# Backward attention: dO times O summed to one column a head group, added to dP group by group on VectorE

## The chip, the cores and the metric

The kernel runs on one core of a Trainium2 chip. The metric is the device time of one execution in microseconds; the time before is the median of three runs. A core has five engines that run side by side, each with its own queue of instructions in a fixed order: TensorE (in the profile PE for its matmuls and PEld for its weight loads), VectorE (DVE), ScalarE (ACT), GpSimd (POOL) and SyncE (SP, which here only issues DMAs). An instruction that needs another engine's result waits for a semaphore, and everything behind it in its engine's queue waits with it. Matmuls write into PSUM, from which VectorE or ScalarE must copy the result out (an evacuation) before the buffer can be used again.

## What is computed

A transformer block, forward and backward in one launch: a LayerNorm with a modulation from a condition vector, an attention with 32 heads over 64 segments of 32 rows with 8 memory rows carried from segment to segment, and a gated feed-forward network. The outputs are the block's output and eleven gradients. The part that matters is the attention of one segment, and its gradient:

```python
q = jnp.einsum('btd,dhe->bhte', h, Wq)
k = jnp.einsum('btd,dhe->bhte', h, Wk)
v = jnp.einsum('btd,dhe->bhte', h, Wv)
scores = jnp.einsum('bhqe,bhke->bhqk', q, k) * scale
scores = jnp.where(mask[None, None], scores, -1000000000.0)
p = _softmax(scores, axis=-1)
o = jnp.einsum('bhqk,bhke->bhqe', p, v)
o = jnp.einsum('bhte,hed->btd', o, Wo)
mem = o[:, :M, :].copy()
...
_out, _vjp = jax.vjp(_f, A_x, A_mem0, A_Wq, A_Wk, A_Wv, A_Wo, B_w_gate, B_w_up, B_w_down, c, w_mod)
_grads = _vjp(grad_out)
```

Going backward, with dO the gradient of a head's output and P its softmax, the gradient of the values is dV = P^T dO. With dP = dO V^T, the gradient of the scores is dS = scale * P * (dP - D), where D is one number for each query row, the sum of dO times O over the row. Then dQ = dS K and dK = dS^T Q. The gradient of the memory rows goes to the segment before, so the 64 segments run one after the other, from the last to the first.

## The kernel before

The kernel runs in stages; the change lies in the one of the backward attention, `phase4`. Its loop takes the 64 segments in turn. The 32 heads are packed three to a group of 120 columns (3 heads of 40 rows), which gives 11 groups, and the groups are worked on in three parts, `pi` = 0, 1, 2, of 4, 4 and 3 groups. A part of 4 groups of 128 columns in float32 is one PSUM bank.

What one segment does, in the order of the code:

- The incoming gradient `dyT` is multiplied with Wo (`col_pass`, L255) and turned (`turn`, L1480) to give dO for each head, `dOT`. `prod` (L1578) multiplies `dOT` into the stored O on VectorE, in place.
- `grad_mm("dVT", ...)` gives the products of dV^T, gv0, gv1 and gv2, one a part; `dp` (L1593) gives dO V^T into `dp_ps`; `dost(2)` transposes the last groups of `dOT`.
- `ds` (L1601) subtracts D: it multiplies the product dO times O by a matrix of minus ones (`negones`), 120 columns wide, into the same PSUM buffer as `dp`, so that each of the 120 columns has D taken off. One instruction of VectorE for each part (L1603) multiplies this by the scale and by P and writes `dS`.
- The head products `dht(dVT, WvT, ...)` (L215) add dV^T times Wv into `dh_ps`. They use the array in strips of 32 columns, four heads side by side. Then follow gv2 and gr0, gr1, gr2, the products of the dV rows, which `rv_out` copies out of PSUM: part 0 and 2 on ScalarE, part 1 on VectorE.
- `dstt(0)` to `dstt(2)` transpose `dS` on TensorE (L1526); part 1 is evacuated by VectorE, 0 and 2 by ScalarE, into `dST`.
- Three products of dK^T (`gks`), evacuated by VectorE into `dKT`, and three of dQ^T, evacuated by ScalarE into `dQT`. Then the head products with Wk (`dht(dKT, WkT, pi)`), the rest of those with Wv, and those with Wq (L223).
- The sums are folded (`fold_split`, `split_pair`, `fold_sum`), which gives the memory gradient that the next segment starts from.

Every fourth segment also evacuates a product of the rows outside the memory into `RBd` on VectorE, ahead of its `ds`, and does a second small transpose in the middle.

Two things set the order of the work. At the end of the loop `self.pin(i0)` ties the instructions of each engine to the order in which the code issues them, so nothing overtakes. And most PSUM tiles of the loop come from one pool, `psp`, with six buffers under one tag; which buffer a tile gets, and so whose evacuation its first matmul has to wait for, is decided by the framework when the program is built. `ps_f32` and `ps_b16` take from it. The pool `psb` holds the long sums `dh_ps` apart from these.

Of the kernel before, what the change touches and what calls it, by code (L numbers as in the profile page):

```python
# [8 lines left out]
F32 = mybir.dt.float32  # L9
AF = mybir.ActivationFunctionType  # L10
ALU = mybir.AluOpType
# [29 lines left out]
class K:  # L41
# [1356 lines left out]
    def phase4(self):  # L1398
        nc, tc, cfg, io = self.nc, self.tc, self.cfg, self.io
        D, DC, H, E, L, M, T, G, NS = cfg.D, cfg.DC, cfg.H, cfg.E, cfg.L, cfg.M, cfg.T, cfg.G, cfg.NS  # L1400
        GW = 128
# [4 lines left out]
        with self.p4_ctx as ctx:  # L1406
            WqT, WkT, WvT, WoT, negones = self.WqT, self.WkT, self.WvT, self.WoT, self.negones
# [4 lines left out]
            sb2 = ctx.enter_context(tc.tile_pool(name="p4s2", bufs=2, reuse_waits="tile"))  # L1412
# [3 lines left out]
            PG = 4  # L1416
            PW = PG * GW

            def ps_f32(name):
                return psp.tile([128, PG, GW], F32, name=name, tag="p")  # L1420
# [23 lines left out]
            def part3(t, pi):  # L1444
                return t[:, pi * PW:min((pi + 1) * PW, G * GW)].rearrange("p (g x) -> p g x", x=GW)
# [75 lines left out]
            def transposes_part(src, pi, w=GW, m=128):  # L1521
                ps = ps_b16("tps")
                n = min(PG, G - pi * PG)
                for j in range(n):
                    g = pi * PG + j
                    nc.tensor.transpose(ps[:, j, 0:m], src[0:m, g * w:g * w + GW], self.ident[0:m, 0:m])  # L1526
                return ps[:, 0:n, 0:m]
# [32 lines left out]
            for s in reversed(range(NS)):  # L1560
# [11 lines left out]
                VT, OT, Pst, Kst, Qst = ld["VT"], ld["OT"], ld["Pst"], Kst_t, Qst_t  # L1572
                dS, dST, dOst = dSs[0], dSTs[0], dOst_t
                dVT, dKT, dQT = dXTs["dVT"][0], dXTs["dKT"][0], dXTs["dQT"][0]
# [13 lines left out]
                def dp(pi):  # L1588
                    ps = dps[pi] = ps_f32("dp_ps")
                    n = min(PG, G - pi * PG)  # L1590
                    for j in range(n):
                        g = pi * PG + j
                        nc.tensor.matmul(ps[:, j, 0:120], lhsT=dOT[:, g * 120:g * 120 + GW], rhs=VT[:, g * GW:g * GW + 120],  # L1593
                                         start=(j == 0), stop=False, skip_group_check=True)

                def ds(pi):
                    ps = dps[pi]
                    n = min(PG, G - pi * PG)
                    for j in range(n):
                        g = pi * PG + j  # L1600
                        nc.tensor.matmul(ps[:, j, 0:120], lhsT=OT[:, g * GW:(g + 1) * GW], rhs=negones[:, 0:120],  # L1601
                                         start=False, stop=True, skip_group_check=True)
                    nc.vector.scalar_tensor_tensor(out=part3(dS, pi)[:, :, 0:120], in0=ps[:, 0:n, 0:120],  # L1603
                                                   scalar=cfg.scale, in1=part3(Pst, pi)[:, :, 0:120],
                                                   op0=ALU.mult, op1=ALU.mult)

                def grad_part(nm, lh, rh, xt, pi, eng):
                    grad_out(nm, xt, pi, eng, grad_mm(nm, lh, rh, pi))

                def grad_mm(nm, lh, rh, pi):  # L1610
                    ps = ps_f32("g_ps")
                    n = min(PG, G - pi * PG)
                    for j in range(n):
                        g = pi * PG + j
                        w = GW if nm == "dV" else 120
                        nc.tensor.matmul(ps[:, j, 0:w], lhsT=lh[:, g * GW:(g + 1) * GW], rhs=rh[:, g * GW:g * GW + w],  # L1616
                                         start=True, stop=True)
                    return ps

                def grad_out(nm, xt, pi, eng, ps):  # L1620
                    self.evac(eng, part3(xt, pi)[:, :, 0:120], ps[:, 0:min(PG, G - pi * PG), 0:120])
                    if pi == NP - 1 and nm != "dVT":
                        rows = rxp.tile([128, G, 128], BF16, name="rows_x")
                        nc.sync.dma_start(rows[:], xt[:, :], transpose=True)
                        dram = {"dKT": self.DKR, "dQT": self.DQR}[nm][s]
                        row_stores.append(lambda: nc.gpsimd.dma_start(dram, rows[:]))
# [3 lines left out]
                def rv_out(pi, eng, ps):  # L1630
                    n = min(PG, G - pi * PG)
                    self.evac(eng, rv_rows[:, pi * PG:pi * PG + n, :], ps[:, 0:n, :])

                def dstt(pi):
                    ps = transposes_part(dS, pi, m=120)
                    self.evac("dve" if pi == 1 else "act", part3(dST, pi)[:, :, 0:120], ps)
# [32 lines left out]
                gv0 = grad_mm("dVT", dOst, Pst, 0)  # L1669
                prod(0)  # L1670
                dp(0)
                prod(1)
                dp(1)
                prod(2)
                dp(2)
                gv1 = grad_mm("dVT", dOst, Pst, 1)
                grad_out("dVT", dVT, 0, "act", gv0)
                if b_done:
                    b_done()
                dost(2)  # L1680
                grad_out("dVT", dVT, 1, "act", gv1)
                ds(0)
                ds(1)
                ds(2)
                self.pop_later()
                dht(dVT, WvT, 0)
# [3 lines left out]
                gr1 = grad_mm("dV", Pst, dOst, 1)  # L1690
# [11 lines left out]
                    dO_tails(s - 1)  # L1702
                grad_out("dVT", dVT, 2, "act", gv2)
                rv_out(0, "act", gr0)
                rv_out(1, "dve", gr1)
                dstt(0)
                rv_out(2, "act", gr2)
                row_stores.append(lambda s=s, rows=rv_rows: nc.gpsimd.dma_start(self.DVR[s], rows[:]))
                dstt(1)
                dstt(2)  # L1710
                gks = [grad_mm("dKT", Qst, dS, pi) for pi in range(NP)]
                load_rows(Qst_t, self.QST, s - 1)
# [22 lines left out]
                g = s // 4  # L1735
# [428 lines left out]
```

## Time and profile before

| | us |
|---|---|
| median of 3 runs (3080.75 to 3086.59) | 3083.49 |
| the profiled execution's own time | 3080.64 |
| its span, first to last instruction | 3078.9 |
| mean granted TensorE clock over the span | 0.991 |
| backward attention loop, first to last row of L1601 | 1539.2 to 2493.1 |
| VectorE's dS (L1603), 192 instructions, busy | 111.4 |
| VectorE's wait ahead of L1603 | 19.2 |
| matmuls of L1601, 704 instructions, each | 0.216 |

The lines of the profile are read like this. A group of instructions has its line in the code, engine, operation, what it writes and reads (`out<-in`), partitions by elements and type, how often, then the busy time in us, the mean length of one in ns, and the idle time of the engine just before them with what ended it. A line of the timeline has start and length in us, and several like instructions in a row are merged into one with their count. Line 63 and line 61 are those of the helper `evac`, so evacuations are told apart by their tiles. Matmuls overlap: each takes 0.216 us from start to end, but the next starts long before that.

### The profile page before, as it was taken

What the parts mean: (1) busy time and instruction counts of PE and PEld (TensorE: products, weight loads), DVE (VectorE), ACT (ScalarE), POOL (GpSimd) and SP (SyncE); (2) the same over time, 40 slices, a digit from 0 to 9 for tenths busy, and PEclk for the clock granted to TensorE, in tenths of its full rate; (3) what the DMA queues carried; (4) which work ended last, traced back from release to release, by engine and by line L of the source; (5) the groups of instructions that cost most, each with busy time, mean ns of one, the idle gap of its engine ahead of it and who ended that gap; (6) DMA issues with size and microseconds to landing.
All of it is one profiled execution on the core that took longest, in us unless ns stands there. A gap on an engine that the chain in (4) does not pass through costs nothing.

```text
span 3078.9 us, 106050 instructions
## 1 busy us (share of the span) xinstructions
PE 2985.9 (97%) x43769; PEld 1821.5 (59%) x43845; DVE 1613.0 (52%) x3799; ACT 1254.4 (41%) x3056; POOL 1386.1 (45%) x2960
## 2 busy tenths in 40 slices
PE   6999999999999799989899999999999999999999
PEld 3666666666665444445577777777777754445455
DVE  4556656665655788742255555555555632322221
ACT  2555555555555433322155555555555520111011
POOL 3666767667766222211244444444444422333322
PEclk8999999999999899999999999999999999999999
DMA  8888788788778799997599999999999998666574
GB/s 300 217 215 204 204 209 217 203 214 212 206 202 255 199 229 231 225 282 254 176 232 246 244 247 246 245 248 244 248 243 245 253 278 278 201 194 221 188 236 149
DMA packets 845992, 703.54 MB, mean 229 GB/s; under 512 B 544354, under 2 KB 717954, under 8 KB 845124
## 3 DMA queue, kind: packets, MB, share of 16 engines
q1 hardware_dynamic: 714196, 486.69, 62.7%
q0 software_dynamic: 60656, 148.64, 15.1%
q10 hardware_dynamic: 70656, 61.41, 6.4%
q8 instruction: 345, 5.65, 0.8%
q14 instruction: 139, 1.14, 0.1%
HBM read 294.93 MB, written 276.35 MB: 186 GB/s over the span
## 4 chain that ended last, share of the span: by engine, by line
PE 45%; issue 3%; POOL 1%; DMA 1%; DVE 0%; ACT 0%; SPq 0%; POOLq 0%
PE gps L1954 9%; PE dh_ps L215 8%; PE g_ps L1616 6%; PE pass_ps L255 5%; PE gps5o L1968 5%; PE dhq_ps L223 4%; PE dh_tps L215 3%; PE dp_ps L1593 2%; PE tps L1526 2%; PE dp_ps L1601 1%; PE turn_ps L1480 1%; PE dh_ft L323 1%; POOL out_dram L1958 1%; DMA dhb<-DHA 0%; PE turn_ps L264 0%
## 5 line engine op out<-in xcount | busy, mean ns | idle before, releaser
L1954 PE MATMUL gps<-rows,hrows 128*128 128x512 bf16 (+2 forms) x2124 | 415.6, 355 | 1.9
L1954 PEld LDWEIGHTS <-hrows 128*128 128x128 bf16 x2160 | 211.3, 98 | 204.5
L255 PEld LDWEIGHTS <-hT 128*32 128x32 bf16 x6144 | 158.3, 97 | 168.5 <-DMA Wq<-in_A_Wq_dram 5.5
L1660 POOL COPY dOst<-RAd 96x512 bf16<-96x512 bf16 x128 | 75.5, 613 | 311.4 <-DVE RAd L63 311.2
L63 DVE CAST ot<-gps 128x512 bf16<-128x512 f32 (+3 forms) x76 | 48.1, 633 | 286.9 <-PE gps L1954 188.4
L1958 POOL DMA_DIRECT2D out_dram<-ot x108 | 81.5, 755 | 255.9 <-DVE ot L63 137.2
L61 ACT ACTIVATE ot<-gps 128x512 bf16<-128x512 f32 (+3 forms) x75 | 41.3, 551 | 352.3 <-PE gps L1954 230.7
L909 POOL TENSOR_TENSOR Pst<-Pst,rden 120x1408 bf16<-120x1408 bf16 x63 | 159.7, 2536 | 47.7 <-issue 21.4
L61 ACT ACTIVATE dVT<-g_ps 128x480 bf16<-128x480 f32 (+1 forms) x192 | 104.7, 545 | 95.5 <-PE g_ps L1616 95.1
L63 DVE CAST RA0v<-pass_ps 128x512 bf16<-128x512 f32 x128 | 88.5, 692 | 91.2 <-PE pass_ps L255 85.3
L255 PE MATMUL pass_ps<-Wv,hT 128*32 128x512 bf16 x2048 | 134.2, 382 | 0.0
L215 PE MATMUL dh_ps<-WvT,dVT 128*32 128x512 bf16 x2048 | 133.4, 380 | 0.3 <-DVE RBd L63 0.2
L255 PE MATMUL pass_ps<-Wq,hT 128*32 128x512 bf16 x2048 | 123.3, 383 | 5.3 <-DMA Wq<-in_A_Wq_dram 5.3
L1968 PE MATMUL gps5o<-WoT,rows 128*128 128x512 bf16 x580 | 127.7, 379 | 0.6
L223 PE MATMUL at_ps<-Wo,OT 128*32 128x256 bf16 x4096 | 124.6, 274 | 3.0 <-DMA Wo<-in_A_Wo_dram 3.0
L255 PE MATMUL pass_ps<-Wk,hT 128*32 128x512 bf16 x2048 | 121.6, 379 | 2.2 <-ACT hT L899 1.1
L255 PE MATMUL pass_ps<-WoT,dyT 128*32 128x256 bf16 (+1 forms) x3072 | 122.4, 308 | 0.9 <-ACT dyT L1734 0.9
L223 PE MATMUL dhq_ps<-WqT,dQT 128*32 128x256 bf16 x4096 | 122.9, 273 | 0.0
L215 PE MATMUL dh_ps<-WkT,dKT 128*32 128x512 bf16 x2048 | 122.3, 380 | 0.0
L223 PEld LDWEIGHTS <-dQT 128*32 128x32 bf16 x4096 | 109.6, 97 | 15.9
L1603 DVE SCALAR_TENSOR_TENSOR dS<-dp_ps,Pst_l 128x480 bf16<-128x480 f32 (+1 forms) x192 | 106.1, 608 | 19.2 <-PE dp_ps L1601 19.2
L223 PEld LDWEIGHTS <-OT 128*32 128x32 bf16 x4096 | 103.8, 97 | 18.6 <-issue 6.5
(421 smaller groups left out, 7034.9 us busy)
## 6 DMA issues: line engine op xcount, KB each, us to landing
OSR<-Ost SPq DMA_DIRECT2D x64, 352.0 KB
OT<-OT SPq DMA_DIRECT2D x64, 352.0 KB
VT<-VTr SPq DMA_DIRECT2D x64, 352.0 KB
PS<-Pst SPq DMA_DIRECT2D x64, 352.0 KB
OT_l<-OT SPq DMA_DIRECT2D x64, 352.0 KB
Pst_l<-PS SPq DMA_DIRECT2D x64, 352.0 KB
VT_l<-VT SPq DMA_DIRECT2D x64, 352.0 KB
DVR<-rows_x POOLq DMA_DIRECT2D x64, 352.0 KB, 6.2
```

The lines of the kernel that those rows point to most:

```text
L61: return nc.scalar.activation(out, in_, AF.Copy)
L63: return nc.vector.tensor_copy(out, in_)
L215: self.nc.tensor.matmul(ps[32 * j:32 * j + 32, :], lhsT=lhsT, rhs=w, start=(n < 4), stop=(n >= total - 4), tile_position=(0, 32 * j))
L223: nc.tensor.matmul(ps[32 * j:32 * j + 32, :], lhsT=x[k], rhs=w[k][:, 256 * d:256 * d + 256], start=(n == 0), stop=(n == total - 1), tile_p ...
L255: self.nc.tensor.matmul(ps[32 * j:32 * j + 32, :], lhsT=lhs(c), rhs=rhs, start=(c == 0), stop=(c == DC - 1), tile_position=(0, 32 * j))
L909: nc.gpsimd.tensor_tensor(Pst[0:120, :, :], Pst[0:120, :, :], rden[:, :].unsqueeze(2).to_broadcast([120, G, 128]), op=ALU.mult)
L1603: nc.vector.scalar_tensor_tensor(out=part3(dS, pi)[:, :, 0:120], in0=ps[:, 0:n, 0:120], scalar=cfg.scale, in1=part3(Pst, pi)[:, :, 0:120], ...
L1616: nc.tensor.matmul(ps[:, j, 0:w], lhsT=lh[:, g * GW:(g + 1) * GW], rhs=rh[:, g * GW:g * GW + w], start=True, stop=True)
L1660: nc.gpsimd.tensor_copy(dOst[0:96, 512 * hf:512 * hf + 512], RAd[0:96, 512 * hf:512 * hf + 512])
L1954: nc.tensor.matmul(ps[:, 0:ng * E], lhsT=hrows[:, tp_, c * 128:(c + 1) * 128], rhs=rows[:, tp_, 0:ng * E], start=(tp_ == 0), stop=(tp_ == ...
L1958: nc.gpsimd.dma_start(outw[c * 128:(c + 1) * 128, h0:h0 + 3 * (ng - 1) + 1:3, :], ot[:, 0:ng * E].rearrange("p (h e) -> p h e", e=E))
L1968: nc.tensor.matmul(pss[gg][:], lhsT=src[0][:, src[1], gg * E:(gg + 1) * E], rhs=dyrows[:, tp_, :], start=(tp_ == order[0]), stop=(tp_ == o ...
```

## The change

`dp` closes its sums. `ds` multiplies by one column of minus ones in place of 120 and puts the result, minus D, into column 120 of each group's part of the same PSUM buffer, which `dp` leaves free. VectorE copies these columns of a part (4, 4 and 3) into a small tile `negD`, and then does one instruction for each of the 11 groups: it adds the group's column of `negD` to dP and multiplies by P. The scale is no longer in `dS`; `grad_out` puts it in as it evacuates dK^T (VectorE) and dQ^T (ScalarE), while dV^T is copied as before. `rv_out(1, "dve", gr1)`, the copy of the second part of the dV rows, is issued after `dstt(1)` in place of before `dstt(0)`.

```diff
                         nc.tensor.matmul(ps[:, j, 0:120], lhsT=dOT[:, g * 120:g * 120 + GW], rhs=VT[:, g * GW:g * GW + 120],
-                                         start=(j == 0), stop=False, skip_group_check=True)
+                                         start=(j == 0), stop=True, skip_group_check=True)
 
                 def ds(pi):
                     ps = dps[pi]
                     n = min(PG, G - pi * PG)
                     for j in range(n):
                         g = pi * PG + j
-                        nc.tensor.matmul(ps[:, j, 0:120], lhsT=OT[:, g * GW:(g + 1) * GW], rhs=negones[:, 0:120],
+                        nc.tensor.matmul(ps[:, j, 120:121], lhsT=OT[:, g * GW:(g + 1) * GW], rhs=negones[:, 0:1],
                                          start=False, stop=True, skip_group_check=True)
-                    nc.vector.scalar_tensor_tensor(out=part3(dS, pi)[:, :, 0:120], in0=ps[:, 0:n, 0:120],
-                                                   scalar=cfg.scale, in1=part3(Pst, pi)[:, :, 0:120],
-                                                   op0=ALU.mult, op1=ALU.mult)
+                    nd = sb2.tile([128, PG], F32, name="negD", bufs=3)
+                    nc.vector.tensor_copy(nd[:, 0:n], ps[:, 0:n, 120])
+                    for j in range(n):
+                        g = pi * PG + j
+                        nc.vector.scalar_tensor_tensor(out=dS[:, g * GW:g * GW + 120], in0=ps[:, j, 0:120],
+                                                       scalar=nd[:, j:j + 1], in1=Pst[:, g * GW:g * GW + 120],
+                                                       op0=ALU.add, op1=ALU.mult)
...
                 def grad_out(nm, xt, pi, eng, ps):
-                    self.evac(eng, part3(xt, pi)[:, :, 0:120], ps[:, 0:min(PG, G - pi * PG), 0:120])
+                    to, src = part3(xt, pi)[:, :, 0:120], ps[:, 0:min(PG, G - pi * PG), 0:120]
+                    if nm == "dVT":
+                        self.evac(eng, to, src)
+                    elif eng == "act":
+                        nc.scalar.activation(to, src, AF.Copy, scale=cfg.scale)
+                    else:
+                        nc.vector.tensor_scalar_mul(to, src, cfg.scale)
...
                 rv_out(0, "act", gr0)
-                rv_out(1, "dve", gr1)
                 dstt(0)
                 rv_out(2, "act", gr2)
                 row_stores.append(lambda s=s, rows=rv_rows: nc.gpsimd.dma_start(self.DVR[s], rows[:]))
                 dstt(1)
+                rv_out(1, "dve", gr1)
                 dstt(2)
```

## The prediction

> **What bounds the kernel now.** I read the page's first part, then the stage of the backward attention loop (1537 to 2495 us) as a table of stretches, then one segment in order of time, engine by engine.
>
> ```profile
> PE 2985.9 (97%) x43769; PEld 1821.5 (59%) x43845; DVE 1613.0 (52%) x3799; ACT 1254.4 (41%) x3056; POOL 1386.1 (45%) x2960
> 1540.00:2490.00 950.00, 946.60 (x19805) 676.78 (x19806) 550.82 (x1386) 502.51 (x1297) 439.23 (x1090) 1.00 0.99 245
> 2006.17:2021.10 14.93, 14.92 (x317) 10.63 (x314) 8.29 (x21) 7.63 (x21) 7.09 (x19) 1.00 0.98 249
> ```
>
> The columns of the last two lines are the stretch, its length, and the busy time of PE, PEld, DVE, ACT, POOL, then clock, DMA share, GB/s. TensorE is busy for 946.6 of 950.0 us at full clock: it is the bound, and whatever makes it wait is paid in full. The whole change lies in this stage, 64 segments of 14.9 us (every fourth 15.6). Inside one segment (start, length in us):
>
> ```profile
> 2008.03 0.74 PE L1601 MATMUL dp_ps<-negones,OT_l 128*128 128x120 bf16 x11
> 2008.76 1.48 PE L215 MATMUL dh_ps<-WvT,dVT 128*32 128x512 bf16 x24
> 2010.17 0.33 PE L1616 MATMUL g_ps<-Pst_l,dOst 128*128 128x120 bf16 x3
> 2010.34 0.78 PE L1616 MATMUL g_ps<-dOst,Pst_l 128*128 128x128 bf16 x11
> 2010.95 0.74 PE L1526 MATMUL tps<-ident,dS 120*128 120x120 bf16 x11
> 2011.55 0.78 PE L1616 MATMUL g_ps<-dS,Qst 128*128 128x120 bf16 x11
> 2012.17 0.91 PE L1616 MATMUL g_ps<-dST,Kst 128*128 128x120 bf16 x11
> 2013.01 1.91 PE L215 MATMUL dh_ps<-WkT,dKT 128*32 128x512 bf16 x32
> 2010.54 0.47 ACT L61 ACTIVATE dVT<-g_ps 128x360 bf16<-128x360 f32 x1 [1.35 <-PE g_ps L1616]
> 2010.91 0.59 ACT L61 ACTIVATE rows_x<-g_ps 128x512 bf16<-128x512 f32 x1
> 2011.38 0.58 ACT L61 ACTIVATE dST<-tps 128x480 bf16<-128x480 bf16 x1
> 2011.84 0.51 ACT L61 ACTIVATE rows_x<-g_ps 128x384 bf16<-128x384 f32 x1
> 2012.21 0.50 ACT L61 ACTIVATE dST<-tps 128x360 bf16<-128x360 bf16 x1
> 2008.44 1.66 DVE L1603 SCALAR_TENSOR_TENSOR dS<-dp_ps,Pst_l 128x480 bf16<-128x480 f32 x3 [0.26 <-PE dp_ps L1601]
> 2010.99 0.69 DVE L63 CAST rows_x<-g_ps 128x512 bf16<-128x512 f32 x1 [0.75 <-PE g_ps L1616]
> ```
>
> See two things. ACT runs five evacuations without a break from 2010.54 to 2012.71 (each starts some 0.11 before the one ahead ends), and the last dQ^T product needs the last of them: 11 matmuls take 0.91 there against 0.74 to 0.78 elsewhere. In this stretch ACT is level with TensorE. And VectorE has only 0.75 us of idle time between dS and the dV rows.
>
> **Names.** gv2: third dV^T product; r0 to r2: the products of the dV rows; t0 to t2: the three transposes of dS; k0 to k2 and q0 to q2: the dK^T and dQ^T products. All share six PSUM buffers.
>
> **The change, part by part.** *Matmuls of one column.* 11 matmuls at L1601 start 52 ns apart ((0.74 - 0.216)/10, 0.216 being one matmul). Nearest row for the new form: the 32-column products of the fold, each with its own full weight load:
>
> ```profile
> 2002.94 0.37 PE L323 MATMUL dh_ft<-foldsel,dST 128*128 128x32 bf16 x8
> 2717.15 0.20 DVE L1999 TENSOR_SCALAR dx_b<-dx_s,rstd 128x1 f32<-128x1 f32 x1
> 2717.27 0.20 DVE L2000 TENSOR_SCALAR dx_c<-dx_s,rstd 128x1 f32<-128x1 f32 x1
> L1167 DVE SCALAR_TENSOR_TENSOR ta<-dxh,rstd,Wk 128x512 f32<-128x512 f32 x8 | 5.9, 743 | 0.0
> L1154 DVE SCALAR_TENSOR_TENSOR dxh<-mm,Wv 128x512 f32<-128x512 f32 x16 | 11.1, 691 | 24.6 <-ACT dh2b L1151 24.6
> L735 DVE RECIPROCAL rden<-or_ps 120x8 f32<-120x8 f32 x64 | 13.3, 208 | 10.8 <-PE or_ps L730 3.9
> L63 DVE COPY dOT<-turn_ps 128x32 bf16<-128x32 bf16 x128 | 15.7, 164 | 0.0
> ```
>
> (0.37 - 0.176)/7 is 27 ns; bounds 25 (that row's smallest spacing) and 52 (no gain); I take 26. Saved: 11 x 26 = 0.29 us a segment, 18 us in all, if nothing waits. But the second half of the dV^T head products (2008.76) already waits for ACT's second dVT evacuation: that ends at 2009.18, its weight loads start at 2009.235, its matmuls at 2009.42. Moved up by 0.29 they would be due at 2009.13 and start at 2009.24: 0.18 is kept. In the segments of 15.6 us the same head products wait for a copy of RBd on VectorE, which this change doesn't move: 0 is kept.
>
> *VectorE.* Removed: three instructions (651, 651, 522 ns; back to back 565, 565, then the last's 522: 1.66). Added: 11 of 120 columns and 3 copies of 4. The old rows rise by 129 ns for 120 columns, so 120 take 522 - 2 x 125 = 272 (1.04 ns a column); the scalar is now a pointer, and L1167 against L1154 prices that at 743 - 691 = 52: 325. Back to back they start 83 ns earlier than their length (565 for 648), so 242 apart; the pair dx_b, dx_c, both with pointers, shows the same overlap (0.12 apart at 0.20). The copy has no row; from below 120 (that spacing), from above 208 (the reciprocal of 8 PSUM columns); I take 153, the 32-column PSUM copy's 164 less 28 columns at 0.5. What reads its result starts 34 ns after its end (reciprocal 208, next 242 later). A block of four: 187 + 4 x 242 = 1.16; the three: 3.22 against 1.66, so 100 us more work for VectorE in all.
>
> A page of the Trainium skill, "VectorE: DVE Perf Modes", section "The DRAIN you can't avoid", says that the next operation waits until the pipe is empty, with or without a semaphore. The trace shows 83 ns of overlap instead. By the page the 11 would cost 325 each and the three blocks some 4.0 us; I follow the rows.
>
> *Scale.* dK^T and dQ^T evacuations multiply by an immediate on the engines that did the copy. The old dS did that too at 651 for 480 columns, and the cast took 653: I take 0, bounds -0.02 and +0.05 each, hidden under the head products (1.91). No DMA is added or removed; SP's and POOL's queues keep their order.
>
> *rv_out(1) moved* behind the second dS transpose on VectorE. It is ready at 2010.99 and would run at 2012.1; what waits for it is POOL's store of the dV rows at 2015.10 and, now, the PSUM buffer of q2. Behind it stand the three dKT evacuations.
>
> *The buffers.* The built programs list what each instruction waits for. The six PSUM buffers are handed out in another order. Before, r2 took the buffer of a dp and t0, t1, t2 those of the last dS, of dh_rb and of dVT. After: r2 waits for ACT's dVT(2); t0 for the last of dS(1); t1 for ACT's rv_out(0); t2 for ACT's evacuation of t0; k1 for ACT's rv_out(2); q1 for ACT's evacuation of t2. Behind each of these waits stand all later matmuls, and behind those ACT's next evacuation: TensorE's chain and ACT's are now threaded through each other, several times a segment. PE to ACT or VectorE costs 0.04, back 0.05 (2010.50 to 2010.54; 2012.71 to 2012.76).
>
> Ordinary segment, by the clock of the lines above. Each start is the later of two: TensorE's turn (r matmuls start 0.056 apart, t, k and q 0.052) and the end of what it waits for plus 0.05; ACT's evacuations keep their lengths and their 0.11 of overlap. gv2 2009.99, done 2010.32; dVT(2) on ACT 2010.36 to 2010.83; rv_out(0) 2010.73 to 2011.32. r2 2010.88 (was 2010.79). VectorE's first copy starts when four one-column matmuls are done (2008.03 + 3 x 0.026 + 0.17 + 0.04 = 2008.32), and dS(1) is ready at 2008.32 + 2 x 1.16 + 0.08 = 2010.72, so t0 goes at 2011.05, done 2011.42. t1 2011.37. ACT's dST(0) 2011.46 to 2012.04, so t2 2012.09 (dS(2) is ready at 2011.63). k0 2012.24; rv_out(2) 2011.92 to 2012.43, so k1 2012.48, k2 2012.69, q0 2012.85; dST(2) 2012.45 to 2012.95; q1 2013.06, q2 2013.27, and the dK^T head products start at 2013.52, not 2013.01. VectorE: free of dS at 2011.54, dh_rb, dST(1) from 2011.78, rv_out(1) 2012.09, dKT from 2012.70 to 2014.36; the heads need its thirds at 2013.52, 2014.17 and 2014.8: covered, by 0.1 to 0.4. So +0.5.
>
> Long segment (every fourth, with the copy of RBd and a second small transpose): there t0 waits for rv_out(0) (2041.62 + 0.05, was 2041.08), t2 for dST(0) (2042.66 + 0.05), q0 for dST(2) (2043.57 + 0.05), and q2 takes q0's buffer, so it waits for ACT's dQT(0): q0 2043.62, done 2043.99, dQT(0) 2044.03 to 2044.60, q2 2044.65, heads 2044.90, not 2043.34: +1.5.
>
> Sum: 49 x 0.5 + 15 x 1.5 = 47 us on the profiled execution's 3080.6: 3128. The median of the runs shown lies 2.9 above it, so 3130.
>
> **Rivals.** (1) *VectorE becomes the bound:* instructions with a pointer don't overlap, 359 apart (325 + 34). Then dS(1) is ready at 2011.54 and dS(2) at 2012.80; t2 ends at 2012.9, dKT starts at 2013.8 and the heads at 2014.5: +1.5, and +2.2 in long ones: 49 x 1.5 + 15 x 2.2 = 106, 3190. Against it: dx_b and dx_c overlap. It decides from about 265 ns apart on, where the 0.3 us between dS(1)'s end and t0 is used up; at 300 apart it adds some 20 us: 3150. (2) *Faster:* the new buffer waits end before TensorE arrives, and the saved columns stay: 49 x 0.18 = 9, to 64 x 0.29 = 18; 3075 to 3065. It needs ACT to be done with t0 by 2011.2 in an ordinary segment; ACT is full from 2010.5 on, which speaks against it. (3) *The column saves nothing,* its weight load setting the pace at 52 ns: 49 x 0.18 more, 3139. (4) *Only part of the threading bites* (ACT's later evacuations find their input early, the long segments gain no third wait): half, 3107.
>
> **How the numbers follow.** Forecast 0.65, with (3) inside it; (1) 0.13; (2) 0.05; (4) 0.15; the rest near no change. Range 3104 to 3152: from (4) to a spacing of 300 ns in (1). What can be told from no change here is about 0.2%, 6 us. Slower 0.93, same 0.03, faster 0.04.
>
> **What would show it.** Right: L1601's eleven within 0.45 us; 11 new VectorE rows of about 325 ns, some 240 apart; TensorE idle ahead of the transposes of dS and the dQ^T products, released by ACT's dST, rows_x and dQT; ordinary segments of 15.4, long ones of 17.1 us. Wrong: idle ended by VectorE's dS or dKT (rival 1), or segments below 14.9 (rival 2). The forecast falls if ACT's evacuations with a scale are slower, or if the clock leaves 1.00 with TensorE's new gaps.

## The result, and the profile after

The changed kernel takes 3128.51 us (median of 4 runs, 3125.89 to 3129.24), against 3082.12 for the kernel before, run beside it (4 runs, 3080.61 to 3086.59). The ratio is 1.0147, 95% interval 1.0129 to 1.0164: slower by 46 us. The profiled execution takes 3129.24 us, 48.6 more than the one of before.

The page's first part, and its row of the new dS (busy us, mean ns, idle before):

```profile
PE 2997.2 (96%) x43845; PEld 1804.3 (58%) x43845; DVE 1711.4 (55%) x4503; ACT 1272.8 (41%) x3056; POOL 1388.2 (44%) x2960
...
L1607 DVE SCALAR_TENSOR_TENSOR dS<-dp_ps,negD,Pst_l 128x120 bf16<-128x120 f32 x704 | 193.7, 336 | 6.8
```

VectorE has 98 us more work and TensorE 11 us more "busy" time, although its matmuls got shorter: a matmul takes some 0.21 us from start to end and the next one starts 0.05 after it, so a wait of up to 0.16 behind it still shows as busy. The loop shows more. From one segment's first RAd copy on VectorE to the next, the four kinds of segment took 15.12, 15.64, 14.88 and 14.99 us before, and take 15.62, 17.21, 15.38 and 15.49 now: 0.50 more in three of four, 1.57 in the long one. First to last that is 1009.41 us against 960.75, so the loop holds the whole loss. TensorE's granted clock over the loop is 1.00 in both.

One ordinary segment of the changed kernel in order of time (start, length; in brackets the idle time ahead and what ended it). Line 1616 of before is now 1620, the evacuation of dQ^T is line 1629, that of dK^T 1631:

```profile
1887.53 0.44 PE L1601 MATMUL dp_ps<-negones,OT_l 128*128 128x1 bf16 x11
...
1888.00 1.09 DVE L1607 SCALAR_TENSOR_TENSOR dS<-dp_ps,negD,Pst_l 128x120 bf16<-128x120 f32 x4
...
1889.66 1.05 PE L1620 MATMUL g_ps<-dOst,Pst_l 128*128 128x128 bf16 x11
1889.86 0.47 ACT L61 ACTIVATE dVT<-g_ps 128x360 bf16<-128x360 f32 x1 [1.19 <-PE g_ps L1620]
...
1890.23 0.59 ACT L61 ACTIVATE rows_x<-g_ps 128x512 bf16<-128x512 f32 x1
...
1890.39 0.84 DVE L1607 SCALAR_TENSOR_TENSOR dS<-dp_ps,negD,Pst_l 128x120 bf16<-128x120 f32 x3
...
1890.55 0.69 PE L1526 MATMUL tps<-ident,dS 120*128 120x120 bf16 x8
1890.96 0.57 ACT L61 ACTIVATE dST<-tps 128x480 bf16<-128x480 bf16 x1
...
1891.58 0.32 PE L1526 MATMUL tps<-ident,dS 120*128 120x120 bf16 x3 [0.34 <-ACT dST L61]
...
1891.74 0.75 PE L1620 MATMUL g_ps<-dS,Qst 128*128 128x120 bf16 x11
...
1892.21 1.66 DVE L1631 TENSOR_SCALAR dKT<-g_ps 128x480 bf16<-128x480 f32 x3
...
1892.33 0.74 PE L1620 MATMUL g_ps<-dST,Kst 128*128 128x120 bf16 x11
...
1893.00 0.98 PEld L215 LDWEIGHTS <-dKT 128*32 128x32 bf16 x24
```

Two waits make the 0.50 (the columns' gain and shorter waits later on come off them). The eleven matmuls of the dV rows take 1.05 instead of 0.78, since the third product waits for ScalarE's third evacuation of dV^T (1889.86 + 0.47). Then the transposes of dS, eleven in one go before, stop after eight: the last three need a PSUM buffer that ScalarE frees at 1891.53, and start at 1891.58. From start to start the first wait adds 0.28 and the second 0.59. Against them stand 0.17 from the shorter columns and 0.20 because the dK^T and dQ^T products, which took 0.78 and 0.91 before, now hardly wait (0.75 and 0.74). The second transpose waits too, for ScalarE's first copy of the dV rows (1890.23 + 0.59 = 1890.82, start 1890.87), but at no cost: the third would wait all the same. In the long segment there are two more waits, ahead of the first transpose and of the third dQ^T product:

```profile
1873.92 0.58 PE L1526 MATMUL tps<-ident,dS 120*128 120x120 bf16 x8 [0.16 <-ACT rows_x L61]
...
1874.94 0.32 PE L1526 MATMUL tps<-ident,dS 120*128 120x120 bf16 x3 [0.45 <-DVE dST L63]
...
1875.82 0.58 PE L1620 MATMUL g_ps<-dST,Kst 128*128 128x120 bf16 x8
1876.28 1.45 ACT L1629 ACTIVATE dQT<-g_ps 128x480 bf16<-128x480 f32 x3 [0.51 <-PE g_ps L1620]
1876.90 0.32 PE L1620 MATMUL g_ps<-dST,Kst 128*128 128x120 bf16 x3 [0.50 <-ACT dQT L1629]
```

(In the second line the copy named as releaser ends just as the transposes start. ScalarE's evacuation of the first transpose ended 0.05 before, at 1874.89, the same distance as in the ordinary segment.)

TensorE's largest waits over the loop, 1540 to 2480 us (us in total, times, longest), are these; before, none of them is there:

```profile
PE tps L1526 <- ACT dST L61: 14.7, 44, 0.3
PE g_ps L1620 <- ACT dQT L1629: 6.5, 13, 0.5
PE tps L1526 <- DVE dST L63: 6.3, 14, 0.4
PE tps L1526 <- ACT rows_x L61: 3.8, 14, 1.6
```

### The profile page after: what moved, and what is told of

It reads as the page before. It is cut to its first block, busy times and chain, and to the rows that moved or that the text cites. A ratio compares the mean times of both kernels' runs of the same rounds, so it can differ in the third digit from the quotient of the medians.

```text
span 3127.4 us, 106754 instructions
## 1 busy us (share of the span) xinstructions
PE 2997.2 (96%) x43845; PEld 1804.3 (58%) x43845; DVE 1711.4 (55%) x4503; ACT 1272.8 (41%) x3056; POOL 1388.2 (44%) x2960
## 3 DMA queue, kind: packets, MB, share of 16 engines
q14 instruction: 145, 1.18, 0.1%
## 4 chain that ended last, share of the span: by engine, by line
PE 44%; DVE 2%; ACT 2%; DMA 1%; issue 1%; POOL 0%; SPq 0%; DVEq 0%; POOLq 0%; ACTq 0%
PE gps L1964 13%; PE dh_ps L215 7%; PE pass_ps L255 4%; PE g_ps L1620 4%; PE gps5o L1978 4%; PE dhq_ps L223 4%; PE dh_tps L215 3%; PE tps L1526 1%; PE dp_ps L1593 1%; DVE dS L1607 1%; PE turn_ps L1480 1%; ACT dST L61 1%; PE dh_ft L323 1%; ACT dVT L61 1%; PE dp_ps L1601 0%
## 5 line engine op out<-in xcount | busy, mean ns | idle before, releaser
L1607 DVE SCALAR_TENSOR_TENSOR dS<-dp_ps,negD,Pst_l 128x120 bf16<-128x120 f32 x704 | 193.7, 336 | 6.8
L215 PE MATMUL dh_ps<-WvT,dVT 128*32 128x512 bf16 x2048 | 140.2, 384 | 3.8 <-DVE RBd L63 3.8
L341 POOL DMA_DIRECT2D DHA<-dh_rb x64 | 34.8, 544 | 224.9 <-DVE dh_rb L337 216.5
```

The costliest lines, as they stand in the source:

```text
L215: self.nc.tensor.matmul(ps[32 * j:32 * j + 32, :], lhsT=lhsT, rhs=w, start=(n < 4), stop=(n >= total - 4), tile_position=(0, 32 * j))
L1607: nc.vector.scalar_tensor_tensor(out=dS[:, g * GW:g * GW + 120], in0=ps[:, j, 0:120], scalar=nd[:, j:j + 1], in1=Pst[:, g * GW:g * GW + 12 ...
```

## The experiments

The question is what lies under these waits. Theory: the PSUM buffers. Rivals: VectorE's longer dS in itself, the scale in the evacuations, the moved copy. For the runs with exchanged buffers the pool is one of six tags with one buffer each, and a written list says which tag each of its 1920 tiles takes:

```diff
-psp = ctx.enter_context(tc.tile_pool(name="p4ps", bufs=6, space=PSUM, reuse_waits="tile"))
+psp = Banks(ctx.enter_context(tc.tile_pool(name="p4ps", bufs=1, space=PSUM, reuse_waits="tile")), BANKS)
...
+    def tile(self, shape, dtype, name, tag):
+        b = self.order[self.n]
+        self.n += 1
+        return self.pool.tile(shape, dtype, name=name, tag="p" + b)
```

**The list itself, a control.** The kernel before with its own buffers written out.

> A control: the kernel before with its own buffers put into a written list. If the list itself costs nothing, 3080 to 3086; any more would have to be taken off the two runs with exchanged buffers.

3082.83 us against 3082.99, ratio 1.0000 (0.9991 to 1.0009): the list costs nothing.

**Before's instructions in the changed kernel's buffers.**

> Before's instructions, every one of them, but each of the 1920 PSUM tiles of the pool is put by a written list into the buffer that it has in the changed kernel. Theory (the waits for PSUM buffers make the loss): TensorE meets the same waits for ACT's evacuations, so nearly the whole loss comes without any of the change's own work: 3128 to 3142, ordinary segments 15.4 to 15.6, long ones 16.9 to 17.3. Rival (VectorE's 100 us of added work make the loss through results that come late): VectorE does no more than before, so 3082. Rival (scale or the moved copy): neither is in it, 3082.

3147.55 us, ratio 1.0206 (1.019 to 1.0222): 63 us lost with none of the change's work, and above the range I gave. The same segment, in its lines of dV rows and dS transposes:

```profile
1893.70 1.05 PE L1616 MATMUL g_ps<-dOst,Pst_l 128*128 128x128 bf16 x11
...
1894.59 0.69 PE L1526 MATMUL tps<-ident,dS 120*128 120x120 bf16 x8
...
1895.62 0.32 PE L1526 MATMUL tps<-ident,dS 120*128 120x120 bf16 x3 [0.34 <-ACT dST L61]
```

These are the changed kernel's two waits, with the same lengths of 1.05, 0.69 and 0.34, although dS is ready long before. The segments of 14.88 take 15.55, which is 0.17 more than in the changed kernel: the columns that this one doesn't save. I had left that out of the estimate. In the segments of 15.12 TensorE also comes to the second dV^T product late, by 0 to 1.8 us (0.2 in the median); the cause is open. So the buffers alone are enough for the loss. It doesn't follow that they are its only cause.

**The changed kernel's instructions in before's buffers.**

> The changed kernel's instructions, with each PSUM tile put by a written list into the buffer that it has in the kernel before. If the other order of buffers were a mere accident of the framework, this would take the loss away: 3065 to 3085. Theory: the order changed because VectorE's longer dS holds the buffers of dP by up to 1.5 us longer; in the old order the third dV-row product and the first transpose of dS wait for just these, so it gets worse than the changed kernel, 3150 to 3185, with TensorE idle released by VectorE's dS. Rival (VectorE's added work counts whatever the buffers): 3128.

3187.01 us, ratio 1.0335 (1.0318 to 1.0352), just above the range. The waits are now VectorE's:

```profile
1907.63 0.75 PE L1526 MATMUL tps<-ident,dS 120*128 120x120 bf16 x11 [0.60 <-DVE dS L1607]
...
1909.32 0.54 PE L1620 MATMUL g_ps<-dS,Qst 128*128 128x120 bf16 x7 [0.73 <-DVE rows_x L63]
```

In the old order the first transpose stands behind the whole of dS, and the dK^T products behind the moved copy. For this dS the framework's new order is thus 58 us better than the old one. That the framework chose it because dS holds its buffers longer fits, but no run shows it.

**Two passes.** dS is made in two passes over a part: dP minus D out of PSUM, then times P in SBUF (`ds` keeps the products and the small copy, into `nds[pi]`). The copy of the dV rows stands where it was before.

```diff
-                    for j in range(n):
-                        g = pi * PG + j
-                        nc.vector.scalar_tensor_tensor(out=dS[:, g * GW:g * GW + 120], in0=ps[:, j, 0:120],
-                                                       scalar=nd[:, j:j + 1], in1=Pst[:, g * GW:g * GW + 120],
-                                                       op0=ALU.add, op1=ALU.mult)
+                def ds1(pi):
+                    n = min(PG, G - pi * PG)
+                    nc.vector.tensor_tensor(part3(dS, pi)[:, :, 0:120], dps[pi][:, 0:n, 0:120],
+                                            nds[pi][:, 0:n].unsqueeze(2).to_broadcast([128, n, 120]), op=ALU.add)
+
+                def ds2(pi):
+                    n = min(PG, G - pi * PG)
+                    nc.vector.tensor_tensor(part3(dS, pi)[:, :, 0:120], part3(dS, pi)[:, :, 0:120], part3(Pst, pi)[:, :, 0:120], op=ALU.mult)
...
                 ds(0)
                 ds(1)
+                ds1(0)
                 ds(2)
+                ds1(1)
+                ds1(2)
+                for pi in range(NP):
+                    ds2(pi)
```

> The one-column sums, their copies and the scale in the evacuations as in the changed kernel, but dS in two passes over a whole part: dP minus D out of PSUM into dS (three instructions, as long as the old dS), then times P in place, in bfloat16, which reads no PSUM; the copy of the dV rows' second part stands where it was before. VectorE's part is some 2.7 us a segment against 3.2 changed and 1.7 before, but the buffers of dP come free about as early as before. Theory: the framework goes back to the old order of buffers, the loss goes, and some of the saved columns stay: 3070 to 3088. Rival (VectorE's added work makes the loss, in proportion): 1.0 of 1.55 us added, so two thirds of 46 us, 3112. Rival (scale): 3128 less nothing.

3080.21 us, ratio 0.9988 (0.9979 to 0.9998). The loss is gone.

```profile
1872.01 0.66 DVE L1609 TENSOR_TENSOR dS<-dp_ps,negD 128x480 bf16<-128x480 f32 x1
1872.65 1.09 DVE L1609 TENSOR_TENSOR dS<-dp_ps,negD 128x480 bf16<-128x480 f32 x2
...
1873.66 0.97 DVE L1614 TENSOR_TENSOR dS<-dS,Pst_l 128x480 bf16<-128x480 bf16 x3
...
1874.29 0.91 PE L1526 MATMUL tps<-ident,dS 120*128 120x120 bf16 x11
```

VectorE's part, from the first small copy to the end of dS, takes 2.82 us (1.66 before, 3.43 changed), and dP's buffers are all free at 1873.74. The transposes run through with a wait of 0.17, as much as the columns save. VectorE's added work thus doesn't count in proportion, which would have been 3112. But I was wrong that the old order of buffers would come back: here the second dK^T product starts 0.05 after ScalarE's evacuation of the first transpose, at 1875.35, and in the kernel before it started before that evacuation ended. So this run changes three things: the time for which dP's buffers are held, dS's end, and the hand-out of the buffers. The next separates the first two.

**Two passes, the second by group.** Eleven short instructions for the second pass, otherwise the same.

```diff
-                    nc.vector.tensor_tensor(part3(dS, pi)[:, :, 0:120], part3(dS, pi)[:, :, 0:120], part3(Pst, pi)[:, :, 0:120], op=ALU.mult)
+                    for j in range(min(PG, G - pi * PG)):
+                        g = pi * PG + j
+                        nc.vector.tensor_tensor(dS[:, g * GW:g * GW + 120], dS[:, g * GW:g * GW + 120], Pst[:, g * GW:g * GW + 120], op=ALU.mult)
```

> As the two passes, but the second pass, in SBUF alone, is done group by group, 11 short instructions: VectorE's part is then some 3.3 us a segment, as long as in the changed kernel, while the buffers of dP are free as early as with the two passes. Theory in its pure form (only the time for which dP's buffers are held counts): 3080 to 3090. Rival (VectorE's work in all counts): 3128. I expect a middle, 3100 to 3118: the buffers are free, but dS comes late for its own first transpose, which now stands behind VectorE; what is above 3085 is the part of the loss that is due to dS itself and not to the buffers.

3115.84 us, ratio 1.011 (1.0093 to 1.0126), in the middle as expected.

```profile
1883.48 1.09 DVE L1609 TENSOR_TENSOR dS<-dp_ps,negD 128x480 bf16<-128x480 f32 x2
...
1884.48 1.52 DVE L1615 TENSOR_TENSOR dS<-dS,Pst_l 128x120 bf16<-128x120 bf16 x11
...
1885.11 1.18 PE L1526 MATMUL tps<-ident,dS 120*128 120x120 bf16 x11
...
1887.67 0.34 PEld L215 LDWEIGHTS <-dKT 128*32 128x32 bf16 x12 [0.19 <-DVE dKT L1637]
```

dP's buffers are free as early as with the two passes, 2.20 us after the start of the eleven sums, but VectorE's part is 0.55 us longer and dS ends at 1886.00. From the sixth on, each transpose starts some 0.05 after the multiply of its own group, so they follow one another at VectorE's 131 ns: the eleven take 1.18, against 0.91 with the two passes and 0.74 before. The dK^T head products then wait 0.09 for VectorE's dKT. An ordinary segment is 0.45 longer than with the two passes, and these two waits for VectorE make 0.33 of it. The rest are waits for PSUM buffers that ScalarE empties. The long segment is 0.86 longer, of which VectorE's late dS makes 0.38 and this wait, which the two-pass kernel doesn't have, 0.51 (over the loop, as in the table above):

```profile
PE g_ps L1626 <- ACT dQT L1635: 6.5, 13, 0.5
```

So the hand-out of the buffers is another one here as well, and the 36 us between the two runs are not the price of VectorE's longer part alone: by these segments some 22 of them are waits for VectorE's results (49 x 0.33 + 15 x 0.38), and some 13 waits for buffers. The theory in its pure form falls, but the split is an estimate.

**The changed kernel with the best buffers I could find.** Only the list.

> The changed kernel's instructions with a written hand-out of the PSUM buffers in which each tile takes the one that came free first, worked out from the times of the changed kernel's trace. Theory in its pure form (an unlucky hand-out makes the loss): 3070 to 3085. What the two passes by group point to: dS itself is late too. In the trace of the changed kernel's ordinary segment the last transpose of dS starts at ScalarE's evacuation of the first, 7.03 us into the segment, and behind that wait stands another, for dS, that would end at 6.73; so a better hand-out can give back some 0.1 to 0.3 us of the 0.5, and up to 0.9 of the 1.6 in long segments: 3108 to 3122.

3112.42 us, ratio 1.01 (1.0086 to 1.0113): it wins 16 us, a third of the loss.

```profile
1886.77 0.84 DVE L1607 SCALAR_TENSOR_TENSOR dS<-dp_ps,negD,Pst_l 128x120 bf16<-128x120 f32 x3
...
1886.90 1.08 PE L1526 MATMUL tps<-ident,dS 120*128 120x120 bf16 x11
...
1888.58 1.65 DVE L1631 TENSOR_SCALAR dKT<-g_ps 128x480 bf16<-128x480 f32 x3
...
1889.29 0.34 PEld L215 LDWEIGHTS <-dKT 128*32 128x32 bf16 x12 [0.20 <-DVE dKT L1631]
```

The wait of the last three transposes is now for dS itself (1886.77 + 0.84 = 1887.61), and after them the dK^T head products wait for VectorE's dKT. The ordinary segment takes 15.29 in place of 15.38, the long one 16.38 in place of 17.21, so most of what is won lies in the long ones. Behind the buffers' waits stand VectorE's, 0.09 away in an ordinary segment. One wait for a buffer that ScalarE empties is left too, 0.11 ahead of the first dK^T product.

**The moved copy, put back in the changed kernel.**

```diff
                 rv_out(0, "act", gr0)
+                rv_out(1, "dve", gr1)
...
                 dstt(1)
-                rv_out(1, "dve", gr1)
```

> The changed kernel with the copy of the dV rows' second part issued where it was before, ahead of the first transpose of dS. Theory: the move is no cause of the loss and was a small gain, since the copy ahead of the dS transposes holds up the evacuation of the second one on a VectorE that is late with dS: 3128 to 3140. Rival (the moved copy, 0.69 us later, holds a PSUM buffer and makes the loss): 3085 to 3110.

3138.69 us, ratio 1.0181 (1.0165 to 1.0196), 10 us more than with the move. The move is no cause of the loss. But neither did the reason I gave come out: in an ordinary segment the added 0.13 stands ahead of the first dQ^T product, which starts 0.05 after ScalarE's evacuation of the third transpose (2023.88 and 2023.93 in one segment). In the changed kernel it started before that evacuation ended, so the wait is for a buffer, handed out otherwise in this run.

**The moved copy alone, in the kernel before.** The same two lines, the other way round.

> The kernel before with the copy of the dV rows' second part moved behind the second transpose of dS, as in the change. The framework hands the PSUM buffers out anew here too (1230 of the 1920 tiles follow the same tile as before). Theory: VectorE is free of dS early here, the copy comes only some 0.3 us later, and the buffer that it holds is met late in the segment: 3084 to 3100. Rival (the move makes the loss): 3115 to 3130.

3110.42 us, ratio 1.0096 (1.0079 to 1.0114): 28 us, between my range and the rival's.

```profile
1887.66 0.58 ACT L61 ACTIVATE dST<-tps 128x480 bf16<-128x480 bf16 x1
...
1887.82 0.99 PE L1616 MATMUL g_ps<-dS,Qst 128*128 128x120 bf16 x11
...
1888.29 0.36 PEld L1616 LDWEIGHTS <-Qst 128*128 128x128 bf16 x6 [0.21 <-issue]
...
1888.67 0.89 PE L1616 MATMUL g_ps<-dST,Kst 128*128 128x120 bf16 x11
```

An ordinary segment is 0.21 longer, and all of it comes ahead of the dQ^T products: the eleven of dK^T take 0.99 for 0.78, because the second product starts only when ScalarE has emptied the buffer of the first transpose (1887.66 + 0.58 = 1888.24, start 1888.29). From the dQ^T products on, TensorE keeps the pace of the kernel before, so the copy that now stands ahead of dKT on VectorE costs nothing there. What is seen is again the new hand-out of the buffers. Some 12 of the 28 us lie in single segments that are longer by up to 3.7 us; their cause is open. What the copy's place costs or saves by itself, with the buffers held fixed, neither of these two runs shows.

**The scale alone.**

```diff
-                                                   scalar=cfg.scale, in1=part3(Pst, pi)[:, :, 0:120],
+                                                   scalar=1.0, in1=part3(Pst, pi)[:, :, 0:120],
...
+                    elif eng == "act":
+                        nc.scalar.activation(to, src, AF.Copy, scale=cfg.scale)
+                    else:
+                        nc.vector.tensor_scalar_mul(to, src, cfg.scale)
```

> The kernel before with the scale taken out of dS and put in at the evacuations of dK^T and dQ^T. Theory: no cost, 3082 to 3085. Rival (the evacuations with a scale are slower by up to 0.05 us, six a segment): up to 19 us more, 3102.

3082.56 us against 3082.42, ratio 1.0 (0.9991 to 1.0009); the segments take 14.88 and 15.64, as before. No cost.

**The one column and its copies, with the three old instructions for dS.**

```diff
-                        nc.tensor.matmul(ps[:, j, 0:120], lhsT=OT[:, g * GW:(g + 1) * GW], rhs=negones[:, 0:120],
+                        nc.tensor.matmul(ps[:, j, 120:121], lhsT=OT[:, g * GW:(g + 1) * GW], rhs=negones[:, 0:1],
...
+                    nd = sb2.tile([128, PG], F32, name="negD", bufs=3)
+                    nc.vector.tensor_copy(nd[:, 0:n], ps[:, 0:n, 120])
```

> The kernel before with the one-column sums and the small copies of the column, but VectorE's three instructions as they were: D is left out of dS. The 11 matmuls shrink by 0.29 us a segment, of which the prediction keeps 0.18 in the 49 ordinary ones: 3074. All kept in all 64: 3065. If the weight load sets the pace: 3083. The copies are 0.3 us of VectorE a segment, beside TensorE's work: no cost.

3077.42 us, ratio 0.9981 (0.9972 to 0.999). The segments of 14.88 take 14.71, those of 15.64 still take 15.64: 0.17 kept in the one, nothing in the other, which makes 8 us; 5.6 are left in the medians. This is what the columns bring when nothing new is waited for.

This run, put beside the changed kernel with the copy back in its place (3138.69), also says what in the change makes the loss. Both have the columns and the small copies, both leave the copy of the dV rows where it was, and the scale costs nothing: what is left between them, 61 us, is the step from three long instructions for dS to eleven short ones. By the timing, the new hand-out of the buffers comes with the same step: here the products from the dV rows to the heads follow one another as in the kernel before, while the other run has the changed kernel's waits ahead of the transposes (its last transpose starts 4.16 us after the first of the eleven sums, as in the changed kernel; here it is 3.28).

## Why the prediction was right, and where it was incomplete

- **The sum.** 47 us were forecast (49 x 0.5 + 15 x 1.5), 48.6 measured between the two profiled executions, with 0.50 and 1.57 a segment; the median of 3128.51 is 1.5 below the 3130.
- **Columns.** The eleven take 0.44 us, so they start 28 ns apart ((0.44 - 0.163)/10) against the forecast's 26. The product behind them comes 0.17 earlier (0.18 forecast), and in long segments nothing is kept.
- **VectorE.** 336 ns an instruction and 250 ns apart, against 325 and 242; a segment's dS with its copies takes 3.43 us against 3.22, and VectorE has 98 us more in all against 100. (The old dS is busy for 106.1 us by the page's row, not for the 111.4 of the table ahead; the small copy takes 152 ns, where the prediction's own terms, 164 less 28 x 0.5, make 150 and not 153.) The 86 ns of overlap that the trace has kept rival 1, which begins at 265, away by a narrow margin. The section "The DRAIN you can't avoid" of the Trainium skill's page "VectorE: DVE Perf Modes", which the prediction cites, also says that an operation that is not held starts earlier. The overlap here agrees with that, so page and rows do not differ on it, and the 4.0 us "by the page" do not follow.
- **Scale.** Zero, as forecast.
- **Buffers.** In the clock of the segment shown (120.50 earlier than the prediction's), the third product of the dV rows was due at 1890.38, the first transpose at 1890.55, the second at 1890.87, the third at 1891.59, the dK^T head products at 1893.02. They came at 1890.39, 1890.55, 1890.87, 1891.58 and 1893.00. The four waits of the long segment came too, at 1.57 for 1.5.
- **Where it was incomplete.** It called VectorE's 100 us covered, by 0.1 to 0.4 us. As built that is so: the first third of dKT ends at 1892.87, 0.13 before its reader. But this cover is made of the very waits that the buffers cause. The prediction set the buffers and VectorE against each other as forecast and rival 1, when they stand one behind the other: of the 46 us a better order of buffers gives back 16 (to 3112), and there VectorE's dS and dKT are what is waited for. With dP's buffers free early but dS as late, 33 are still lost; of the 36 against the two-pass kernel some 13 go to buffers again. The kernel that loses nothing has a VectorE part that lets go of PSUM early and also ends early; its buffers are handed out in an order of their own, and what that order contributes was not separated. That the loss comes from the step to eleven short instructions is shown (61 us), and the new hand-out comes with it. Why the framework then picks this order is not shown; a moved copy alone also makes it pick another.
- **The moved copy.** The prediction gave it no price. The changed kernel is 10 us faster with it, through a wait for a buffer.

The two-pass kernel is the fastest of those with the whole of dS: 0.12% below the kernel before, with an interval that ends at 0.02%. The hand-out used in the best-buffers run comes from a simple rule, and a better one is not ruled out.

## What to carry to other kernels

Where a small pool of PSUM buffers is shared, an instruction that reads PSUM costs what it takes until its buffer is free again, and the bill comes from whichever engine's evacuation the next owner of a buffer must then wait for; read what each product waits for in the built program, not in the diff. When a wait has been found, ask what ends next behind it: here a second bound lay 0.09 us away in the ordinary segment, so a better order of buffers gave back a third. A small edit can have all buffers handed out anew: as long as the hand-out is not pinned by a list, a difference between two kernels can be the hand-out's and not the edit's. To split a long PSUM operation by group multiplies its fixed time (3.43 us against 1.66 here); a pass that empties PSUM in few large instructions, and a second one in SBUF, ended without loss, at 3080.21 us.

## What the runs showed of the hardware that was not expected

- A bfloat16 multiply in SBUF of 120 columns starts 131 ns after the one before (11 in 1.52 us, each 0.21), against 250 ns for the one out of PSUM with a pointer as its scalar (0.34 each): the overlap is the same, some 85 ns, for long and short ones (the old dS, 648 ns long, starts 565 apart).
- The same move of one copy on VectorE goes with 28 us more in one kernel and 10 us less in the other; in both, TensorE's waits are for PSUM buffers that ScalarE empties.
